# Attention inputs loaded into all 128 partitions, with heads grouped by parity

## The chip, the cores and the metric

The kernel runs on one core of a Trainium2 chip, from Python code that places every instruction on an engine: TensorE (PE) multiplies, ScalarE (ACT) and VectorE (DVE) move and compute, GpSimd (POOL) does some element-wise work, and SyncE (SP) issues the DMAs. The metric is the device time of one launch in microseconds, the median of three runs.

## The reference, cut to what matters

Two attentions, then two mixture-of-experts layers (batch 4, 8 heads, 576 tokens, head size 64, 32 packed queries; 8 experts, width 512, hidden 1024). Everything is float32.

```python
def sm_attn(qq, kk, vv):
    s = scale * np.matmul(qq, kk.transpose(0, 1, 3, 2))
    a = np.exp(s - np.max(s, axis=-1, keepdims=True))
    a = a / (np.sum(a, axis=-1, keepdims=True) + 1e-09)
    return np.matmul(a, vv)
p_packed = sm_attn(p, k, v)              # attention 1: 32 packed queries over 576 tokens
out = sm_attn(q, p_packed, p_packed)     # attention 2: 576 tokens over the 32 packed rows
x = out.transpose(0, 2, 1, 3).reshape(B * S, H * D)
# layer 1: expert = argmax(x @ w_gate); per expert, at most `capacity` tokens:
#   y = relu(x @ w1[e]) @ w2[e], times the token's gate
# layer 2: a second choice of expert with two gates, y = relu(x @ w1b[e]) @ w2b[e]
```

## The kernel before, in words

**Loads.** For each batch, q, k and v come in two halves of four heads each, called G 0 and 1 (`load`, L250). A half is a tile `r` of 96 partitions: partition p holds six consecutive tokens (`R = 6`) of each of the four heads, so a half is 384 pieces of 1536 bytes, 576 KB in all, and there are 24 halves. They rotate through nine buffers (`qkv`). `load_p` brings the packed queries p, 64 KB per batch, and GpSimd copies them next to themselves (`dup_p`). All loads go through SP's queue, which issues in program order and waits there for a free buffer; each load also waits until the load eight places ahead of it has landed.

**Transposes.** `transp` (L257) turns a half of q or k from [96, head, token, d] to [128 = (token parity u, d), 4 heads, 288]: twelve TensorE transposes of [96, 128] into PSUM, then two ACT copies (`evac`, L236) to a tile `T`. For q the copy also reorders columns, so it writes with a step of three elements. `T` has four buffers, one half each.

**Scores.** `score` (L285) makes, for one half, [128 = (4 heads, 32 packed), 2, 288] as eight small matmuls: 64 rows (one token parity) by 32 columns (one head), so that eight tiles of the PE array work side by side. The moving operand is a contiguous run of 288 columns of `T`. A float32 matmul is two instructions in the trace. `s1_mm` does it for k with the packed queries (`pT`), `s2_mm` for q with the packed rows (`ppT`).

**Attention 1's second product.** `s1_exp` writes the weights `a1`, one tile per half. `a1_T` transposes them in six pieces of [128, 96] per half and evacuates on ACT (half 0) or DVE (half 1). `pp_mm` (L326) multiplies with v: 24 matmuls per half of 96 rows by 32 columns with 64 moving columns, four array tiles side by side.

**The rest.** `pp_scale`, `pp_T` normalise and transpose the packed rows; `s2_tr` to `s2_back` are the second softmax, on DVE, POOL and ACT; `g1_*`, `ga` to `gd` choose experts. `moe1_load1` (L491) fetches the chosen expert's w1 as eight loads of 64 partitions (two per 256 columns, one per group of four heads); `moe1_ppw` multiplies it with the packed rows.

**Order.** The order on every engine is written out by hand. `att_iter(b)` runs scores 1 of batch b, the rest of batch b - 1, softmax 2 of batch b - 2. Iterations 0, 1 and 2 are followed by `att_last` (the last scores and the gating of batch 0) and `att_end` (the rest of the last batch, between whose pieces the first expert layer of slot 0 is put). The choice of the first expert, `e0`, is ready near the end of `att_last`; SP then issues w1. Then come the expert layers of two slots, long streams of PE matmuls of 288 or 512 columns.

Of the kernel before, what the change touches and what calls it, by code (L numbers as in the profile page):

```python
# [28 lines left out]
def tile_kernel(  # L29
# [21 lines left out]
    KP = 96  # L51
    R = S // KP
    J = R // 2
    HS = S // 2
# [45 lines left out]
    zt = const.tile([KP, 128], FP32, name="zt")  # L100
# [54 lines left out]
    # ================= gating: pieces =================  # L155
# [3 lines left out]
    def onehot(L, nm, V=nc.vector):  # L159
        """of the logits L [128,n,E]: bf16 one-hot of the first largest, and L less its largest; in two pieces"""  # L160
# [17 lines left out]
    def denom(ex, nm):  # L178
        """1 / (softmax sum + 1e-9)"""
# [7 lines left out]
    def counts(K16, dst):  # L187
        """dst [1,n,E] = kept tokens of each of n batches per expert"""
# [9 lines left out]
    def primary(c, nm, pe, mu, ne, V=nc.vector):  # L198
        """of the counts c [1,n,E]: the index of the largest, more than one?, any?"""
# [50 lines left out]
    def load(b, nm, gs=(0, 1)):  # L250
        src = {"k": k, "q": q, "v": v}[nm]
        for G in gs:
            t = qkv_p.tile([KP, 4, R, D], FP32, tag="r", name="r")
            nc.sync.dma_start(t, src[b, 4 * G:4 * G + 4].rearrange("h (p r) d -> p h r d", r=R))
            raws[nm, b, G] = t

    def transp(b, nm, G, eng=0):  # L257
        """[96, 4 heads, row, d] -> [128 (row parity, d), 4 heads, 288]"""
        src = raws.pop((nm, b, G))
        t = t_p.tile([128, 4, HS], FP32, tag="T", name="T")  # L260
        for hh in range(2):
            ps = psm("tp")
            for u in range(2):
                for j in range(J):
                    tr(nc, ps[:, u, j * KP:(j + 1) * KP], src[:, 2 * hh + u, 2 * j:2 * j + 2, :].rearrange("p r d -> p (r d)"),
                       ident[:KP, :KP])
            i = ps[:, :, 0:HS]
            o = t[:, 2 * hh:2 * hh + 2, :]
            if nm == "q":
                o = o.rearrange("x u (p j) -> x u j p", j=J)  # L270
                i = i.rearrange("x u (j p) -> x u j p", j=J)
            evac(eng, o, i)
        T[nm, b, G] = t

    def make_pT(b):
        pT = ab_p.tile([128, 2, 128], FP32, tag="pT", name="pT")
        ps = psm("pTp")
        for G in range(2):
            tr(nc, ps[:, G, 0:128], p_sb[b][:, G].rearrange("p u d -> p (u d)"), ident)
        nc.scalar.activation(out=pT, in_=ps[:, :, 0:128], func=ACTF.Copy, scale=scale)  # L280
        T["p", b] = pT

    def score(lhs, rhs):
        """lhs(u, hq) [64,32], rhs [128, 4, 288] -> psum [128 (hq, pack), u, 288]"""
        s = psm("s")  # L285
# [14 lines left out]
    def s1_exp(b, G):  # L300
        a1 = at_p.tile([128, 2, HS], FP32, tag="a1", name="a1")
        if G == 0:
            at["sm", b] = as_p.tile([128, 2], FP32, tag="sm", name="sm")
        nc.scalar.activation(out=a1, in_=at.pop(("s1", b, G))[:, :, 0:HS], func=ACTF.Exp,
                             bias=at.pop(("nb", b, G)), accum_out=at["sm", b][:, G:G + 1])
        at["a1", b, G] = a1
# [6 lines left out]
    def a1_T(b, G, eng=0):  # L313
        a1 = at.pop(("a1", b, G))
        ps = psm("a1Tp")
        for u in range(2):
            for j in range(J):
                tr(nc, ps[:KP, u, j * 128:(j + 1) * 128], a1[:, u, j * KP:(j + 1) * KP], ident)
        t = at_p.tile([KP, 2, J, 128], FP32, tag="a1T", name="a1T")
        evac(eng, t, ps[:KP, :, 0:J * 128].rearrange("p u (j n) -> p u j n", j=J))  # L320
        at["a1T", b, G] = t

    def pp_mm(b, G):
        if G == 0:
            at["pp", b] = psm("pp")
        pp, t, vt = at["pp", b], at.pop(("a1T", b, G)), raws.pop(("v", b, G))  # L326
        for u in range(2):
            for j in range(J):
                for hq in range(4):
# [881 lines left out]
```

## Time and profile before

| | |
|---|---|
| time, median of 3 runs | 290.99 us (290.71 to 292.66) |
| span of the profiled execution | 289.3 us |
| PE busy | 259.8 us (90%), 2401 matmuls |
| DVE, ACT, POOL busy | 131.1, 105.4, 44.6 us |
| DMA | 37.16 MB; 50.2% of 16 engines' span |
| packets | 33828, of which 30464 are under 2 KB |

The profiled execution shows only its span, from the first to the last instruction. The median lies 1.7 us above it. A slice of the page is 7.23 us long. A busy PE is not a PE at its peak, since matmuls overlap and the clock may be at half.

### The profile page before, as it was taken

To read this page: it belongs to the slowest core of one execution; us is meant where nothing else is said; L and a number is where in the kernel's file an instruction comes from. 1 tells how busy PE (TensorE), PEld (TensorE's weight loads), DVE (VectorE), ACT (ScalarE), POOL (GpSimd) and SP (SyncE) were. 2 spreads that over 40 slices of the span, in tenths; PEclk is the share of its full clock that TensorE was granted. 3 is DMA by queue.
4 is the path that set the end of the run, shared out by engine and by line. 5 is a ranking of instruction groups with operands and counts; after the bars stand their busy time and mean duration, and the time that the engine had idled before them with its cause. 6 is when DMAs were issued, how large, how long until landed. Compare 5 with 4: busy or idle time off the path is not lost. (4 is left out here: it accounts for less than half of the span.)

```text
span 289.3 us, 5848 instructions
## 1 busy us (share of the span) xinstructions
PE 259.8 (90%) x2401; PEld 226.1 (78%) x2401; DVE 131.1 (45%) x316; ACT 105.4 (36%) x160; POOL 44.6 (15%) x69
## 2 busy tenths in 40 slices
PE   7785949969699898999979999999999999999990
PEld 5565739546479877997879999999888899998870
DVE  0230543858779948617972133359422053640000
ACT  2583537466435412125641224116232143431000
POOL 5000113315415206000533000000010000000100
PEclk9996975998889999999979999999999999999997
DMA  7999999990794000299378622502701181000111
GB/s 176 234 245 199 220 230 239 237 230 9 173 254 160 0 2 0 98 215 227 98 210 227 228 75 72 147 0 76 217 36 54 39 268 61 2 0 36 59 39 44
DMA packets 33828, 37.16 MB, mean 128 GB/s; under 512 B 4224, under 2 KB 30464, under 8 KB 33792
## 3 DMA queue, kind: packets, MB, share of 16 engines
q1 hardware_dynamic: 33792, 36.69, 50.2%
q8 instruction: 21, 0.34, 0.5%
q14 instruction: 15, 0.12, 0.1%
HBM read 31.25 MB, written 4.72 MB: 124 GB/s over the span
## 5 line engine op out<-in xcount | busy, mean ns | idle before, releaser
L21 PE MATMUL o<-w2bh,h 128*128 128x512 f32 x144 | 45.9, 391 | 0.0
L21 PE MATMUL y<-h,w2ah 128*128 128x288 f32 x256 | 44.6, 296 | 0.0
L21 PEld LDWEIGHTS y<-h,w2ah 128*128 128x128 f32 x256 | 37.6, 189 | 0.0
L562 DVE SCALAR_TENSOR_TENSOR h<-h 128x576 fp32r<-128x576 f32 (+3 forms) x64 | 25.8, 446 | 23.6 <-ACT h L555 23.6
L555 ACT ACTIVATE h<-h 128x576 fp32r<-128x576 f32 x32 | 20.4, 650 | 35.0 <-PE h L21 31.2
L25 PE MATMUL tp<-ident,r 96*128 96x96 f32 x192 | 24.1, 290 | 10.0 <-DMA r<-in_q_dram 8.0
L25 PEld LDWEIGHTS tp<-ident,r 96*128 96x128 f32 x192 | 21.8, 172 | 13.5 <-issue 11.0
L21 PEld LDWEIGHTS o<-w2bh,h 128*128 128x128 f32 x144 | 26.9, 188 | 5.7
L21 PE MATMUL o<-w2bl,h 128*128 128x512 f32 x80 | 31.3, 391 | 0.0
L236 ACT ACTIVATE T<-tp 128x576 f32<-128x576 f32 x32 | 24.0, 805 | 19.4 <-PE tp L25 19.2
L21 PE MATMUL y<-h,w2al 128*128 128x288 f32 x128 | 27.6, 297 | 0.7 <-DVE w2al L480 0.7
L21 PE MATMUL h<-yh,w1bh 128*128 128x288 f32 x128 | 27.5, 296 | 0.0
L21 PE MATMUL h<-yh,w1bl 128*128 128x288 f32 x128 | 27.4, 295 | 0.0
L21 PE MATMUL h<-yl,w1bh 128*128 128x288 f32 x128 | 27.3, 295 | 0.0
L21 PEld LDWEIGHTS y<-h,w2al 128*128 128x128 f32 x128 | 20.5, 188 | 1.5 <-DVE w2al L480 1.0
L480 POOL TENSOR_TENSOR w2al<-wraw,w2ah 128x1024 fp32r<-128x1024 f32 x6 | 14.2, 2392 | 44.1 <-DMA wraw<-in_moe_w_dram 26.3
L21 PEld LDWEIGHTS h<-yh,w1bh 128*128 128x128 f32 x128 | 20.6, 189 | 0.2
L21 PEld LDWEIGHTS h<-yh,w1bl 128*128 128x128 f32 x128 | 20.6, 188 | 0.0
L21 PEld LDWEIGHTS h<-yl,w1bh 128*128 128x128 f32 x128 | 20.6, 188 | 0.0
L661 POOL TENSOR_SCALAR osb<-osb,g 64x512 f32<-64x512 f32 x2 | 3.1, 1572 | 110.8 <-DVE osb L660 110.8
L571 ACT ACTIVATE yh<-y 128x576 fp32r<-128x576 f32 x8 | 5.2, 652 | 40.6 <-PE y L21 40.6
L653 ACT ACTIVATE osb<-o,g 128x512 f32<-128x512 f32 x8 | 5.5, 691 | 36.8 <-PE o L21 24.2
(173 smaller groups left out, 387.0 us busy)
## 6 DMA issues: line engine op xcount, KB each, us to landing
wraw<-in_moe_w_dram SPq DMA_DIRECT2D x24, 512.0 KB, 4.8
r<-in_k_dram SPq DMA_DIRECT2D x8, 576.0 KB, 12.4
r<-in_q_dram SPq DMA_DIRECT2D x8, 576.0 KB, 16.4
r<-in_v_dram SPq DMA_DIRECT2D x8, 576.0 KB, 16.4
wraw<-in_moe_w_dram SPq DMA_DIRECT2D x16, 256.0 KB, 5.4
out_dram<-zt SPq DMA_DIRECT2D x2, 1152.0 KB, 7.6
out_dram<-osb SPq DMA_DIRECT2D x8, 256.0 KB, 2.1
a2s<-a2T SPq DMA_DIRECT2D x1, 576.0 KB, 4.9
```

The lines of the kernel that those rows point to most:

```text
L21: return nc.tensor.matmul(out, lhsT=lhsT, rhs=rhs, start=start, stop=stop)
L25: return nc.tensor.transpose(out, in_, ident)
L236: nc.scalar.activation(out=o, in_=i, func=ACTF.Copy)
L480: lo_eng.tensor_tensor(lo, s, hi.bitcast(FP32), op=ALU.subtract)
L555: nc.scalar.activation(out=hi, in_=ps[:, :, 0:HS], func=ACTF.Relu)
L562: nc.vector.scalar_tensor_tensor(o, i, 0.0, a.bitcast(FP32), op0=ALU.max, op1=ALU.subtract)
L571: nc.scalar.activation(out=half(y[0][:, c, :]), in_=ps[:, :, 0:HS], func=ACTF.Copy)
L653: nc.scalar.activation(out=o[:n], in_=ps[:n, 0, :], func=ACTF.Copy, scale=g2[:n, t:t + 1])
L661: nc.gpsimd.tensor_scalar(o[:n], o[:n], g2[:n, t:t + 1], None, op0=ALU.mult)
```

## The change

k and q: a load is now [128, 18, 64]. Partition (h, x) holds 18 of the 36 tokens of block x of head h, one run of 4608 bytes; the two loads of a batch are the two halves of each block, so each holds all eight heads. v: partition (g, p) with g the parity of the head and p a block of nine tokens; a load has four heads, two per parity, in runs of 2304 bytes. Loads keep their number, bytes and place in the program; there are twelve buffers.

A half of q or k is nine transposes of [128, 128], copied contiguously (640 and 512 columns). `T` is one tile per batch and operand, with two buffers. Its columns are (token pair, head, block), so the moving operand of a score, one head's 288 pairs, is read with a step of 128 elements (512 bytes). Every score reads both halves. Heads are grouped by parity: G is now the parity, head = 2 hq + G.

`a1` is one tile for both parities, written by `s1_exp` with a step of two elements. `a1_T` makes nine transposes of [128, 128] per batch, in parts of five and four, whose stationary operand is read with a step of nine elements, and which need both parities. `pp_mm` has 72 matmuls of 64 rows by 32 columns per batch instead of 48 of 96 rows; eight array tiles work side by side.

w1 of the first expert layer is four loads of 128 partitions instead of eight of 64, and `wg_sb` one load instead of two. Comments are removed.

```diff
-    KP = 96
-    R = S // KP
+    ZP = 96
+    BL = 128 // H
+    R = S // BL
     J = R // 2
+    VP = 64
+    VR = S // VP
@@ load_consts
-        for g in range(2):
-            nc.sync.dma_start(
-                wg_sb[64 * g:64 * g + 64], wg1[256 * g:256 * g + 256].rearrange("(q d) e -> d q e", d=64))
+        nc.sync.dma_start(wg_sb, wg1.rearrange("(c p) e -> p c e", p=128))
@@ pools
-    qkv_p = apool("qkv", 9)
-    t_p = apool("t", 4)
+    qkv_p = apool("qkv", 12)
+    t_p = apool("t", 2)
+    a1t_p = apool("a1t", 1)
@@ load_p
-        nc.sync.dma_start(t[:, :, 0, :], p[b].rearrange("(g q) n d -> (q n) g d", g=2))
+        nc.sync.dma_start(t[:, :, 0, :], p[b].rearrange("h (x y) d -> (h x) y d", y=2))
@@ load, transp
-            t = qkv_p.tile([KP, 4, R, D], FP32, tag="r", name="r")
-            nc.sync.dma_start(t, src[b, 4 * G:4 * G + 4].rearrange("h (p r) d -> p h r d", r=R))
+            t = qkv_p.tile([128, J, D], FP32, tag="r", name="r")
+            if nm == "v":
+                nc.sync.dma_start(
+                    t.rearrange("p (q r) d -> p q (r d)", q=2),
+                    v[b, 4 * a:4 * a + 4].rearrange("(q g) (p r) d -> (g p) q (r d)", g=2, r=VR))
+            else:
+                nc.sync.dma_start(
+                    t, (k if nm == "k" else q)[b].rearrange("h (x r) d -> (h x) r d", r=R)[:, J * a:J * a + J, :])
-        t = t_p.tile([128, 4, HS], FP32, tag="T", name="T")
-                    tr(nc, ps[:, u, j * KP:(j + 1) * KP], src[:, 2 * hh + u, 2 * j:2 * j + 2, :].rearrange("p r d -> p (r d)"),
-                       ident[:KP, :KP])
+            T[nm, b] = t_p.tile([128, J, 128], FP32, tag="T", name="T")
+        pair = src.rearrange("p (j u) d -> p j (u d)", u=2)
+        for r0, r1 in ((0, 5), (5, VR)):
+            ps = psm("tp").rearrange("p u n -> p (u n)")
+            for r in range(r0, r1):
+                tr(nc, ps[:, (r - r0) * 128:(r - r0 + 1) * 128], pair[:, r], ident)
+            evac(eng, t[:, VR * a + r0:VR * a + r1, :].rearrange("p r x -> p (r x)"), ps[:, 0:(r1 - r0) * 128])
@@ score, s1_mm
-                mm(nc, s[32 * hq:32 * hq + 32, u, 0:HS], lhs(u, hq), rhs[64 * u:64 * u + 64, hq, :], True, True)
+                mm(nc, s[32 * hq:32 * hq + 32, u, 0:HS], lhs(u, hq), rhs(u, hq), True, True)
+        pT, kT = T["p", b], T["k", b].rearrange("p j (h x) -> p h x j", h=H)
+            lambda u, hq: kT[64 * u:64 * u + 64, 2 * hq + G])
@@ s1_exp, a1_T, pp_mm
+            at["a1", b] = at_p.tile([128, 2, HS, 2], FP32, tag="a1", name="a1")
+        nc.scalar.activation(out=at["a1", b][:, G].rearrange("p c u -> p u c"), in_=at.pop(("s1", b, G))[:, :, 0:HS],
+        a1 = at["a1", b].rearrange("p g c u -> p (g c u)").rearrange("p (x r) -> p r x", r=VR)
+        for r in range(r0, r1):
+            tr(nc, ps[:, (r - r0) * 128:(r - r0 + 1) * 128], a1[:, r], ident)
+        for r in range(*PARTS[i]):
+            for hq in range(4):
+                for G in range(2):
+                    g = slice(64 * G, 64 * G + 64)
+                    mm(nc, pp[32 * hq:32 * hq + 32, G, 0:D], t[g, r, 32 * hq:32 * hq + 32], vt[hq // 2][g, hq % 2, r, :],
+                       r == 0, r == VR - 1)
@@ moe1_load1
-            for G in range(2):
-                nc.sync.dma_start(
-                    w[64 * G:64 * G + 64],
-                    w1a[bass.ds(e, 1), 256 * G:256 * G + 256, fq * 256:(fq + 1) * 256].rearrange(
-                        "o (q d) f -> d (o q) f", d=64),
-                )
+            nc.sync.dma_start(
+                w, w1a[bass.ds(e, 1), :, fq * 256:(fq + 1) * 256].rearrange("o (q p) f -> p (o q) f", p=128))
```

Where the program's order and waits move, two places show it. The first is SP's queue, from the loads of batch 1's q and v on (`DMAHW` is the landing of the load eight ahead, `PE` a buffer that TensorE must have read). Before:

```order
L254 DMA r<-in_q_dram 96x4x384 [waits DMAHW2_49,PE_49]
L254 DMA r<-in_v_dram 96x4x384 [waits DMAHW3_49,PE_49]
L254 DMA r<-in_v_dram 96x4x384 [waits DMAHW4_49,PE_49]
L254 DMA r<-in_q_dram 96x4x384 [waits DMAHW5_49,PE_49]
L244 DMA p_sb<-in_p_dram 128x2x64 [waits DMAHW6_49,Pool_49]
L254 DMA r<-in_k_dram 96x4x384 [waits DMAHW7_49,PE_49]
```

And now:

```order
L262 DMA r<-in_q_dram 128x1152 [waits DMAHW1_49]
L258 DMA r<-in_v_dram 128x2x576 [waits DMAHW2_49]
L258 DMA r<-in_v_dram 128x2x576 [waits DMAHW3_49]
L262 DMA r<-in_q_dram 128x1152 [waits DMAHW4_49,PE_49]
L248 DMA p_sb<-in_p_dram 128x2x64 [waits DMAHW5_49,PE_49,Pool_49]
L262 DMA r<-in_k_dram 128x1152 [waits DMAHW6_49,PE_49]
```

The first load that needs a buffer back from TensorE moves from the first half of batch 1's q to its second half, three loads later.

The second place is PE's queue in iteration 1, from the second part of batch 0's `a1_T` to its product with v. Before (`a_295` is `a1`, `s` scores 1 of batch 1, `tp` batch 0's second half of q, `pp` the product):

```order
L25 MATMUL a1Tp<-ident,a_295 96x128 [waits Activation_49]
L25 MATMUL a1Tp<-ident,a_295 96x128 x5
L21 MATMUL s<-T,pT 32x288 [waits Activation_49]
L21 MATMUL s<-T,pT 32x288 x7
L25 MATMUL tp<-ident,r 128x96 [waits DMAHW1_49,Activation_49]
L25 MATMUL tp<-ident,r 128x96 x5
L25 MATMUL tp<-ident,r 128x96 [waits Activation_49]
L25 MATMUL tp<-ident,r 128x96 x5
L21 MATMUL pp<-r,a1T 32x64 [waits DMAHW7_49,DVE_49]
L21 MATMUL pp<-r,a1T 32x64 x23
L21 MATMUL pp<-r,a1T 32x64 [waits DMAHW0_49]
L21 MATMUL pp<-r,a1T 32x64 x23
```

And now:

```order
L25 MATMUL a1Tp<-ident,a_276 128x128 [waits Activation_49]
L25 MATMUL a1Tp<-ident,a_276 128x128 x3
L21 MATMUL s<-T,pT 32x288 [waits Activation_49]
L21 MATMUL s<-T,pT 32x288 x7
L25 MATMUL tp<-ident,r 128x128 [waits DMAHW1_49,Activation_49]
L25 MATMUL tp<-ident,r 128x128 x4
L25 MATMUL tp<-ident,r 128x128 [waits DVE_49]
L25 MATMUL tp<-ident,r 128x128 x3
L21 MATMUL pp<-r,a1T 32x64 [waits DMAHW7_49,Activation_49]
L21 MATMUL pp<-r,a1T 32x64 x3
L21 MATMUL pp<-r,a1T 32x64 [waits DMAHW0_49]
L21 MATMUL pp<-r,a1T 32x64 x67
```

The steps stand in the same order. Transposes are fewer and wider, the product has 72 matmuls instead of 48, and it waits for the second load of v after its fourth matmul instead of its twenty-fourth.

## Rows read from the trace of the kernel before

**Rows 1.** Page, part 2: 40 slices of the span; granted clock in tenths, GB/s.

```profile
PEclk9996975998889999999979999999999999999997
...
GB/s 176 234 245 199 220 230 239 237 230 9 173 254 160 0 2 0 98 215 227 98 210 227 228 75 72 147 0 76 217 36 54 39 268 61 2 0 36 59 39 44
```

**Rows 2.** Stretches: PE, PEld, DVE, ACT, POOL busy us (count), clock, DMA share, GB/s.

```profile
0.00:65.00 65.00, 50.21 (x768) 38.61 (x769) 23.58 (x56) 33.04 (x56) 12.97 (x50) 0.86 1.04 223
75.00:82.00 7.00, 5.41 (x72) 3.02 (x73) 5.01 (x13) 2.56 (x4) 3.27 (x4) 0.76 1.08 219
...
159.00:161.00 2.00, 2.00 (x17) 2.00 (x16) 0.34 (x1) 0.00 (x0) 0.00 (x0) 1.00 1.00 342
```

**Rows 3.** Waits of PE, 0 to 72 us: who, total us, times, longest.

```profile
PE tp L25 <- DMA r<-in_q_dram: 8.0, 2, 4.3
PE pp L21 <- issue: 2.3, 1, 2.3
PE tp L25 <- DMA r<-in_k_dram: 1.9, 2, 1.0
...
PE pTp L25 <- POOL p_sb L248: 1.0, 1, 1.0
```

**Rows 4.** Timeline, iterations 0 and 1: start, us, engine, line, what, count [idle before].

```profile
5.73 2.15 PE L25 MATMUL tp<-ident,r 96*128 96x96 f32 x12 [1.01 <-DMA r<-in_k_dram]
...
9.22 2.16 PE L25 MATMUL tp<-ident,r 96*128 96x96 f32 x12 [0.90 <-DMA r<-in_k_dram]
...
11.30 2.06 PE L21 MATMUL s<-T,pT 64*32 64x288 f32 x32
...
17.12 0.82 PE L25 MATMUL a1Tp<-ident,a 128*96 128x128 f32 x6
...
24.78 2.15 PE L25 MATMUL tp<-ident,r 96*128 96x96 f32 x12 [3.75 <-DMA r<-in_q_dram]
...
26.86 2.79 PE L21 MATMUL pp<-r,a1T 96*32 96x64 f32 x96
```

**Rows 5.** Timeline, iteration 2 to the first loads of w1.

```profile
34.62 0.72 PE L21 MATMUL s<-T,pT 64*32 64x288 f32 x16
...
35.26 1.21 PE L25 MATMUL tp<-ident,r 96*128 96x96 f32 x12
...
42.10 2.15 PE L25 MATMUL tp<-ident,r 96*128 96x96 f32 x12 [4.29 <-DMA r<-in_q_dram]
...
47.39 2.13 PE L25 MATMUL tp<-ident,r 96*128 96x96 f32 x12
...
49.73 1.62 PE L25 MATMUL tp<-ident,r 96*128 96x96 f32 x12
...
58.01 0.88 PE L21 MATMUL pp<-r,a1T 96*32 96x64 f32 x48
...
64.57 1.52 PE L25 MATMUL a1Tp<-ident,a 128*96 128x128 f32 x6
...
72.57 1.45 SPq L498 DMA_DIRECT2D wraw<-in_moe_w_dram  x2
```

**Rows 6.** A stretch after the first wait for q; columns as rows 2.

```profile
25.00:30.00 5.00, 5.00 (x110) 4.61 (x110) 0.28 (x2) 2.54 (x4) 0.29 (x1) 0.50 0.92 150
```

**Rows 7.** ACT's copies of k (first), q (second): count, min/median/max ns.

```profile
L236 ACT ACTIVATE T<-tp x4: 645/652/652, 48.6 to 51.5; 128x576 f32<-128x576 f32 x4
...
L236 ACT ACTIVATE T<-tp x2: 957/962/966, 19.3 to 20.1; 128x576 f32<-128x576 f32 x2
```

**Rows 8.** Timeline of PE in the first expert layer of slot 1.

```profile
159.84 0.42 PE L21 MATMUL y<-h,w2al 128*128 128x288 f32 x2
160.10 0.69 PE L21 MATMUL y<-h,w2ah 128*128 128x288 f32 x4
160.63 0.43 PE L21 MATMUL y<-h,w2al 128*128 128x288 f32 x2
```

**Rows 9.** Waits of PE's weight loads, 72 us to the end.

```profile
PEld ppw L21 <- DMA wraw<-in_moe_w_dram: 2.3, 3, 1.1
```

More of the change, by code (lines that the diff above doesn't have):

```diff
@@ L99, in tile_kernel @@
         nc.gpsimd.memset(iob[:, b:b + 1], float(b))
-    zt = const.tile([KP, 128], FP32, name="zt")
+    zt = const.tile([ZP, 128], FP32, name="zt")
     nc.gpsimd.memset(zt, 0.0)
@@ L248, in dup_p, with load @@
         nc.gpsimd.tensor_copy(p_sb[b][:, :, 1, :], p_sb[b][:, :, 0, :])
-    def load(b, nm, gs=(0, 1)):
-        src = {"k": k, "q": q, "v": v}[nm]
-        for G in gs:
-            t = qkv_p.tile([KP, 4, R, D], FP32, tag="r", name="r")
-            nc.sync.dma_start(t, src[b, 4 * G:4 * G + 4].rearrange("h (p r) d -> p h r d", r=R))
-            raws[nm, b, G] = t
-    def transp(b, nm, G, eng=0):
-        src = raws.pop((nm, b, G))
-        t = t_p.tile([128, 4, HS], FP32, tag="T", name="T")
[L261 to L264, printed above, removed]
-                    tr(nc, ps[:, u, j * KP:(j + 1) * KP], src[:, 2 * hh + u, 2 * j:2 * j + 2, :].rearrange("p r d -> p (r d)"),
-                       ident[:KP, :KP])
[L267 to L273, printed above, removed]
+    def load(b, nm, pieces=(0, 1)):
+        for a in pieces:
+            t = qkv_p.tile([128, J, D], FP32, tag="r", name="r")
[6 more added lines that the diff above has]
+                    t, (k if nm == "k" else q)[b].rearrange("h (x r) d -> (h x) r d", r=R)[:, J * a:J * a + J, :])
+            raws[nm, b, a] = t
@@ L275, in make_pT @@
     def make_pT(b):
-        pT = ab_p.tile([128, 2, 128], FP32, tag="pT", name="pT")
+        pT = ab_p.tile([128, H, 2, NP // 2], FP32, tag="pT", name="pT")
         ps = psm("pTp")
-        for G in range(2):
-            tr(nc, ps[:, G, 0:128], p_sb[b][:, G].rearrange("p u d -> p (u d)"), ident)
-        nc.scalar.activation(out=pT, in_=ps[:, :, 0:128], func=ACTF.Copy, scale=scale)
+        for y in range(2):
+            tr(nc, ps[:, y, 0:128], p_sb[b][:, y].rearrange("p u d -> p (u d)"), ident)
@@ L281, in make_pT @@
+        nc.scalar.activation(
+            out=pT.rearrange("p h y x -> p y h x"), in_=ps[:, :, 0:128].rearrange("p y (h x) -> p y h x", h=H),
+            func=ACTF.Copy, scale=scale)
         T["p", b] = pT
@@ L300, in s1_exp @@
     def s1_exp(b, G):
[L301 removed]
         if G == 0:
+            at["a1", b] = at_p.tile([128, 2, HS, 2], FP32, tag="a1", name="a1")
             at["sm", b] = as_p.tile([128, 2], FP32, tag="sm", name="sm")
[L304 to L306 removed]
+        nc.scalar.activation(out=at["a1", b][:, G].rearrange("p c u -> p u c"), in_=at.pop(("s1", b, G))[:, :, 0:HS],
+                             func=ACTF.Exp, bias=at.pop(("nb", b, G)), accum_out=at["sm", b][:, G:G + 1])
     def s1_rs(b):
@@ L311, in s1_rs, with a1_T, pp_mm @@
         nc.vector.reciprocal(sm, sm)
[L313 to L324, printed above, removed]
-            at["pp", b] = psm("pp")
[L326 to L329, printed above, removed]
-                    mm(nc, pp[32 * hq:32 * hq + 32, G, 0:D], t[:, u, j, 32 * hq:32 * hq + 32],
-                       vt[:, hq, 2 * j + u, :], u == 0 and j == 0, u == 1 and j == J - 1)
+    PARTS = ((0, 5), (5, VR))
+    def a1_T(b, i, eng=0):
+        if i == 0:
+            at["a1T", b] = a1t_p.tile([128, VR, 128], FP32, tag="a1T", name="a1T")
+        r0, r1 = PARTS[i]
+        a1 = at["a1", b].rearrange("p g c u -> p (g c u)").rearrange("p (x r) -> p r x", r=VR)
+        ps = psm("a1Tp").rearrange("p u n -> p (u n)")
+        for r in range(r0, r1):
+            tr(nc, ps[:, (r - r0) * 128:(r - r0 + 1) * 128], a1[:, r], ident)
+        evac(eng, at["a1T", b][:, r0:r1].rearrange("p r x -> p (r x)"), ps[:, 0:(r1 - r0) * 128])
+    def pp_mm(b, i):
+        if i == 0:
+            at["pp", b] = psm("pp")
+        pp, t = at["pp", b], at["a1T", b]
+        vt = [raws["v", b, a].rearrange("p (q r) d -> p q r d", q=2) for a in range(2)]
+        for r in range(*PARTS[i]):
[4 more added lines that the diff above has]
+                       r == 0, r == VR - 1)
     def pp_scale(b):
```

17 lines of the change are left out of this document (11 added, 6 removed).

## The prediction, made before the changed kernel ran

> **What bounds the kernel now.** I read the page's 40 slices first [rows 1]. The loads run flat at about 200 to 245 GB/s in the first nine slices and then stop, while the clock dips in slices 4, 6 and 7 and again around 11. From about 75 us on the clock stays at nines. So there are two kernels in one: an attention that runs beside a saturated load queue, and an expert part in which PE has work all the time. The stretches say how saturated [rows 2]: 0 to 65 us has a DMA share of 1.04 and only 223 GB/s. 24 loads of 589,824 bytes and four p of 64 KB are 14.4 MB; at 223 GB/s that is 65 us, the whole stretch.
>
> Next the waits of PE up to 72 us [rows 3]: 8.0 us for q in two waits, 2.3 us ahead of the product with v (an "issue" wait, where v of batch 2 is the operand still missing), 1.9 us for k, 1.0 us for p. That is 13.2 us. [...]
>
> **The loads.** The same 16 engines at the same share reach very different rates: 223 GB/s at 1.04 for pieces on 96 partitions, 219 at 1.08 for w1 on 64 partitions, 342 at 1.00 for weights on 128 partitions, although those pieces are shorter (1 KB) [rows 2]. No row shows pieces of 2304 or 4608 bytes from memory, so the rate lies between no gain (223) and 342 or somewhat more; I take 342, the row with the same number of partitions. Then a load takes 1.72 us instead of 2.6, and all 14.4 MB take 42 us instead of 65.
>
> *Start.* The first load lands 0.9 us earlier, so the transposes of 5.73 us start at 4.83, and those of 9.22 at 7.4, where PE gets there and not the load. Scores now need both copies of k, one more copy of 0.65 us [rows 7]. So the scores of 11.30 us start at 7.4 + 2.08 + 0.65 = 10.1, 1.15 us earlier; the wait for p (0.95 in the timeline) goes as well. Iteration 1 (17.12 us, rows 4) starts 2.1 us earlier.
>
> *Waits for q and v.* 3.75 and 4.29 us [rows 4, 5] and 2.3 us [rows 3] go, if the loads are in time. Taking 3.1 us as the first load's start of transfer (4.83 - 1.72): the eighth load lands at 17.3 us and is wanted at 18.9; the fourteenth at 27.8, wanted at 29.8; v of batch 2 (the nineteenth) at 36.6, wanted at 43.9; the last at 45, wanted at 54. The margins close at about 315 GB/s; at 280 the fourteenth is 3.5 us late and the later ones are not later than that. SP no longer holds these back: the first load that wants a buffer from PE is three places later, and deeper buffers leave the rest well ahead.
>
> *Half clock.* After the first wait: 2.15 - 1.21 for 12 transposes, 2.79 - 2 x 0.88 for the product [rows 4, 5], and 0.2 for two small transposes (estimate), 2.2 us. After the second: the transposes of 42.10, 47.39 and 49.73 us give back 0.94 + 0.92 + 0.41 [rows 5], the product the same 1.03 (it has the same 96 instructions), small ones 0.5 (estimate), 3.8 us. After the third, six transposes at 64.57 us take 1.52 instead of 0.82 [rows 4, 5]: 0.7 us.
>
> Sum: 2.1 + 3.75 + 2.2 + 4.29 + 3.8 + 2.3 + 0.7 = 19.1 us.
>
> *w1.* Eight loads of 64 partitions become four of 128: 2.1 MB at 342 instead of 219 GB/s, 6.1 instead of 9.6 us. In slot 0 the weight loads of PE wait 2.3 us for w1 [rows 9]; I take 1.0 of it, since DVE's and ACT's work for the last batch stands next to these waits. In slot 1 no wait on w1 shows, and nothing is gained. The shorter SP queue gains nothing either.
>
> **PE's own work, which is now the bound.** *Transposes of q and k:* 24 narrow ones per operand and batch took 2 x 1.21 us; 18 wide ones, by six wide ones in 0.82 us [rows 4], take up to 2.46. I take no change. *`a1_T`:* 12 become 9, 1.64 becomes 1.23 us, so -1.6 us over four batches. The strided stationary operand has no row; its bounds are nothing and a doubling of the 1.23 us (+4.9 in all). I take nothing, since weight loads lie beside other matmuls. *`pp_mm`:* 144 instructions per batch instead of 96. At the present pace, 48 in 0.88 us [rows 5], that is 2.64 instead of 1.76 us; if eight tiles side by side finish twice as many as four, it is 1.3. So -0.4 to +0.9 per batch; I take +0.6, near the upper end, because 64 columns are so short that the number of instructions counts, +2.4 in all.
>
> *Strided scores.* This is the unknown. 16 scores of 16 instructions each take 0.72 us now [rows 5]. A stream of 288 columns alone takes 0.79 / 6 = 0.13 us [rows 8]. If the step of 512 bytes costs nothing, a score stays at 0.72. If the tiles could no longer read side by side at all, it is 16 x 0.13 = 2.1 us. The nearest row with a step is another engine's: ACT's copies of q write with a step of 12 bytes and take 962 instead of 652 ns [rows 7], 1.5 times. If each stream takes 1.5 to 2 times 0.13 us and the tiles still overlap, a tile's two streams end 0.13 to 0.26 us later. I take +0.25 per score, 4.0 in all, with 0 and 22 us as bounds.
>
> [...]
>
> *ACT.* 16 copies of q lose 0.31 us each, 5.0 us; eight `s1_exp` write with a step and may gain as much each, at most 2.5 us. I cost both at nothing: the second `s1_exp` of a batch is followed by k's transposes before `a1_T` wants it. Without that cover it is 0.3 us for each of four batches. *New waits:* with loads early, PE meets ACT, DVE and POOL more often, whose copies and second softmax had slack during the waits for q. I allow 1.5 us (estimate: a score's 0.72 us for each of two iterations).
>
> **Sum.** 19.1 + 1.0 - (2.4 - 1.6) - 4.0 - 1.5 = 13.8 us. The expert part behind it moves as a whole. The span goes from 289.3 to 275.5; with the 1.7 us between the span and the median of the runs, 277.
>
> **Rivals.** *A, the strided read halves the score's pace:* a score takes 1.44 instead of 0.72 us, as if only half of the tiles could read at once. 16 x 0.72 = 11.5 instead of 4.0, and the time is 284.7. For it: eight tiles draw on the same rows of memory at once, four of them on the same 64 partitions. Against it: the present 0.72 us is mostly start and end of the streams. [...]
>
> *B, the loads don't get faster:* 223 GB/s is what this stream from memory can do. Then only w1's and PE's small terms move and the time stays within 1%, about 290. For it: no row has 14 MB in one go at 342. Against it: the share of 1.04 at 223 says the engines are busy and slow, while 1.00 goes with 342.
>
> *C, slower:* the tiles of a score read one after the other. Without the strided term the gain is 17.8 us; it is used up when a score takes 0.72 + 17.8 / 16 = 1.83 us. At 2.1 us, with 16 instructions in a row at 0.13, the price is 22 us and the time 295. [...] Against it: the row with a step loses a factor of 1.5, not three.
>
> *D, better than forecast:* the strided read is free and no new waits come, 271.5; with eight tiles also faster in the product, 267.5.
>
> **Chances.** The forecast, with a range of its own of 270 to 283 (the lower end without strided price, the upper end with the loads at 280 GB/s): 0.62. A 0.15, D below 270 0.14, B 0.05, C 0.04. A run of this kernel tells about 1% from no change, so faster means below 288.1: forecast, A and D, 0.91. Within 1%: B, 0.05. Slower: C, 0.04. The range of 266 to 287 leaves out B, C, the upper part of A and the lower part of D, under 0.2.
>
> **What would show it.** In the profile after: the stretch of loads ends near 45 us at about 340 GB/s; no wait of PE for q or v over 1 us and a clock of 1.00 from 20 to 60 us; iteration 1 starts near 15 us and w1 is issued near 55 to 60 us (72.57 now); a score of 16 instructions takes 0.9 to 1.0 us; 72 product matmuls take about 2.3 us a batch. The prediction is wrong if a score takes over 1.4 us, if the loads stay under 280 GB/s, or if PE waits for ACT or DVE by more than 3 us in an iteration.

## The result, and the profile after

The changed kernel takes 279.99 us (279.18 to 280.06), the kernel before 291.83 us beside it; the ratio is 0.961 (95% 0.955 to 0.966). 277.0 was forecast, within 266 to 287. The profiled execution has a span of 278.1 us, 11.2 less than before; 13.8 less were forecast. Two profiles further down, of runs for k and of the loads of 64 partitions, are of the longest execution of their kernels (277.5 and 289.7 us), so lengths read from them lean long.

The page's slices after (the rows that answer to [rows 1]):

```profile
PEclk9999999998899999999799999999999999999998
...
GB/s 220 386 328 332 401 394 32 5 5 215 241 154 0 2 0 49 307 206 75 210 158 302 125 78 101 52 0 162 142 45 49 53 303 26 4 0 38 61 40 45
```

The loads take six slices instead of nine, at 220 to 400 GB/s, and the dips of the clock at 20 to 55 us are gone; eights stay in slices 10 and 11 (63 to 76 us). By stretches (columns as in [rows 2]):

```profile
0.00:43.00 43.00, 37.20 (x597) 23.79 (x597) 14.69 (x35) 24.16 (x45) 9.77 (x46) 1.00 0.94 338
30.00:35.00 5.00, 5.00 (x62) 2.40 (x51) 3.78 (x8) 1.59 (x3) 1.12 (x1) 1.00 1.03 408
```

At the DMA share that gave 223 GB/s before [rows 2], 408 are moved; the mean from 0 to 43 us is 338. The waits of PE in the first 75 us (compare [rows 3]):

```profile
PE ppTp L25 <- DVE pps L349: 1.8, 1, 1.8
PE tp L25 <- DMA r<-in_k_dram: 1.7, 2, 1.5
PE s L21 <- ACT T L240: 1.5, 2, 0.8
PE s L21 <- issue: 1.3, 1, 1.3
PE gp L21 <- issue: 1.2, 1, 1.2
...
PE ppw L21 <- DMA wraw<-in_moe_w_dram: 0.2, 1, 0.2
```

No wait for q is left, and v and p are not waited for. But two waits called "issue" stand there, 2.5 us together. The timeline of PE (compare [rows 4, 5]):

```profile
4.89 1.95 PE L25 MATMUL tp<-ident,r 128*128 128x128 f32 x9 [0.17 <-DMA r<-in_k_dram]
8.54 1.17 PE L25 MATMUL tp<-ident,r 128*128 128x128 f32 x9 [1.49 <-DMA r<-in_k_dram]
10.56 2.64 PE L21 MATMUL s<-T,pT 64*32 64x288 f32 x32 [0.84 <-ACT T L240]
...
16.08 0.74 PE L25 MATMUL a1Tp<-ident,a 128*128 128x128 f32 x5
17.47 1.42 PE L21 MATMUL s<-T,pT 64*32 64x288 f32 x16 [0.66 <-ACT T L240]
18.83 1.20 PE L25 MATMUL tp<-ident,r 128*128 128x128 f32 x9
...
31.16 0.85 PE L25 MATMUL a1Tp<-ident,a 128*128 128x128 f32 x5
...
37.42 1.66 PE L21 MATMUL pp<-r,a1T 64*32 64x64 f32 x144
...
47.09 0.84 PE L25 MATMUL a1Tp<-ident,a 128*128 128x128 f32 x5
```

A score takes 1.42 us where it took 0.72. The product has 144 instructions in 1.66 us, where 96 took 2 x 0.88. Iteration 1 starts at 16.08 (17.12 before), iteration 2 at 31.16 (33.83), the last scores' stage at 47.09 (54.41), and the first matmul of the expert layers at 70.35 (81.07). So the first stage is 1.0 us shorter, iteration 1 1.6, iteration 2 4.7, the last stage 3.4, the experts 0.5: 11.2 us in all.

### The profile page after: what moved, and what is told of

It reads as the page before. It is cut to its first block, busy times and chain, and to the rows that moved or that the text cites. A ratio compares the mean times of both kernels' runs of the same rounds, so it can differ in the third digit from the quotient of the medians.

```text
span 278.1 us, 6072 instructions
## 1 busy us (share of the span) xinstructions
PE 258.7 (93%) x2533; PEld 218.1 (78%) x2533; DVE 130.7 (47%) x316; ACT 100.8 (36%) x160; POOL 44.7 (16%) x69
## 4 chain that ended last, share of the span: by engine, by line
PE 79%; DVE 10%; DMA 4%; ACT 2%; issue 2%; SPq 1%; POOL 0%; ACTq 0%; DVEq 0%; POOLq 0%
PE h L21 23%; PE o L21 18%; PE y L21 17%; PE s L21 7%; PE tp L25 4%; DMA r<-in_k_dram 2%; PE pp L21 2%; DVE eq L206 2%; PE l L21 2%; DVE h L572 2%; PE lp L21 1%; PE a1Tp L25 1%; DMA wraw<-in_moe_w_dram 1%; PE ppw L21 1%; ACT T L240 1%
## 5 line engine op out<-in xcount | busy, mean ns | idle before, releaser
L240 ACT ACTIVATE T<-tp 128x640 f32<-128x640 f32 (+1 forms) x32 | 19.0, 652 | 15.0 <-PE tp L25 15.0
L25 PEld LDWEIGHTS tp<-ident,r 128*128 128x128 f32 x144 | 16.5, 146 | 8.7 <-issue 2.9
L25 PE MATMUL tp<-ident,r 128*128 128x128 f32 x144 | 19.7, 284 | 1.7 <-DMA r<-in_k_dram 1.7
```

The costliest lines, as they stand in the source:

```text
L25: return nc.tensor.transpose(out, in_, ident)
L240: nc.scalar.activation(out=o, in_=i, func=ACTF.Copy)
```

## The experiments

Two questions come out of this. Is it the step of 512 bytes that doubled the score, and what would its return bring? And what are the waits called "issue", one of which the prediction had put down to v? The theory: the step alone makes the score slow, the partitions alone make the loads fast, and PE waits for its own code. All kernels are edits of the changed one. The median of the kernel before was 290.1 to 292.1 us beside them, so times and ratios to before compare to about 1%: 0.961 is the changed kernel's ratio, and 0.962 when it was run again with the last experiments.

One thing moves a time whatever the edit. From the first expert matmul to the end, where the work is the same, the two profiles of the changed kernel take 207.8 and 205.6 us. TensorE waits 2.38 us for DVE at 134 us in both; behind that wait the granted clock is 0.50 for some 3 us in the first profile and 1.00 in the second:

```profile
136.50:139.50 3.00, 3.00 (x13) 3.00 (x14) 2.40 (x11) 1.16 (x3) 0.00 (x0) 0.50 0.99 255
136.50:139.50 3.00, 3.00 (x25) 3.00 (x24) 2.12 (x11) 1.44 (x3) 0.20 (x1) 1.00 0.95 246
```

Seven of the fourteen profiles have it (the kernel before among them; expert part 207.6 to 209.0 us), seven don't (205.6 to 205.9). So less than about 2 us between two profiles is not yet an effect of an edit.

### Runs of 16 columns for all scores

```diff
-        pT, kT = T["p", b], T["k", b].rearrange("p j (h x) -> p h x j", h=H)
+        pT, kT = T["p", b], T["k", b].rearrange("p j (h x) -> p h j x", h=H)
@@ s1_exp
-   out=at["a1", b][:, G].rearrange("p c u -> p u c"), in_=s[:, :, 0:HS]
+   out=at["a1", b][:, G].rearrange("p (x j) u -> p u j x", j=J), in_=s[:, :, 0:HS].rearrange("p u (j x) -> p u j x", j=J)
@@ the same for qT in s2_mm, and in s2_back
+   a2T[:, b, G].rearrange("p (x n jj u) -> p u n jj x", n=NB2, jj=2, u=2)
```

> The scores read T in another column order: 16 columns that lie side by side (one head's blocks of one token pair), then a step to the next pair, so that 18 runs of 64 bytes replace 288 columns at a step of 512 bytes. The new order is undone where the weights are written: s1_exp writes runs of a1 with a step of 144 bytes between elements, s2_back writes a2T by pieces. Theory (the 512-byte step is what makes a score 1.43 us): a score of 16 instructions falls to 0.72 to 0.85 us, and the 16 scores give back 16 x 0.6 to 0.7 = 9.6 to 11.4 us; the time is 269 to 272 against 280, a little above if the writes of s1_exp (0.78 to 0.96 us now) get longer. Rival 1 (it is not the step but the larger tile, read by two operands' halves, or that both halves must be there): the score stays at 1.4 us, and the time at 280. Rival 2 (PE's own score is no longer what sets the iteration): the score falls, but waits of PE for ACT or DVE take the place of it, and the time is 277 to 280.

277.46 us, ratio 0.960 (0.938 to 0.981). The score is back, the time hardly. Timeline of PE:

```profile
16.66 0.72 PE L21 MATMUL s<-T,pT 64*32 64x288 f32 x16 [0.61 <-ACT T L240]
...
24.85 0.72 PE L21 MATMUL s<-T,ppT 64*32 64x288 f32 x16
27.88 0.20 PE L21 MATMUL gp<-wg_sb,ppT 64*32 64x8 f32 x3 [2.29 <-issue]
...
29.49 1.21 PE L21 MATMUL s<-T,pT 64*32 64x288 f32 x16
30.64 2.09 PE L25 MATMUL tp<-ident,r 128*128 128x128 f32 x9
```

and, from 10 to 70 us, DVE's and ACT's groups that write by the new order (count, busy us, mean ns):

```profile
L400 DVE STREAM_TRANSPOSE a2T<-sT 128x576 f32<-128x576 f32 x4 | 4.8, 1190 | 0.0
```

```profile
L312 ACT ACTIVATE a<-s,nb 128x576 f32<-128x576 f32 x8 | 10.4, 1318 | 1.8 <-DVE nb L305 1.8
```

0.72 us ahead of the wait at 27.9 us, as before the change [rows 5]: the step is the whole cause of the doubling, and rival 1 falls. The gain goes into three things. The wait called "issue" in iteration 1 grows from 1.2 to 2.3 us. After it PE is slow for some microseconds (2.09 us for nine transposes that take 1.20, 1.21 us for a score; the mean granted clock of the execution is 0.972, against 0.984 in the changed kernel). And the strides come back on the other engines: `s1_exp` from 0.85 to 1.32 us, `s2_back` from 0.80 to 1.19, and TensorE's waits for them grow: 2.2 instead of 0.5 us behind the last transposes for DVE, 0.9 us instead of none for `s1_exp`. That is rival 2 in its time and in a part of its cause: the wait called "issue" and the slow stretch were not in it.

### Runs for k alone, and an `s1_exp` that reads with the step

The first kernel undoes only k's part of the edit above (k scores in runs, q's with the step).

> The same for the eight scores of k alone; those of q keep the step of 512 bytes. Theory: the k scores fall to 0.72 to 0.85 us, the q scores stay at 1.43, and half of the gain appears, 4.8 to 5.7 us, 274 to 275. Rival (the k scores are covered by waits elsewhere, and q's set the time, or the reverse): a gain of less than 2 us, or nearly the whole of what both bring.

275.67 us, ratio 0.953 (0.930 to 0.976). The k scores take 0.72 us and q's 1.42; iterations 1 and 2 last 13.8 and 14.9 us instead of 15.1 and 15.9. Half of the edit brings as much as the whole, as far as the intervals tell. The second kernel also turns the order of `s1_exp`'s elements:

```diff
-   out=at["a1", b][:, G].rearrange("p (x j) u -> p u j x", j=J), in_=s[:, :, 0:HS].rearrange("p u (j x) -> p u j x", j=J)
+   out=at["a1", b][:, G].rearrange("p (x j) u -> p x j u", j=J), in_=s[:, :, 0:HS].rearrange("p u (j x) -> p x j u", j=J)
```

> Like the kernel with runs of 16 columns for k's scores, but s1_exp puts its elements in the other order: it writes a1 in its own order without a step and reads the scores in PSUM with a step. There s1_exp took 1.32 us writing with steps of 144 bytes, against 0.85 us in the changed kernel (steps of 8 bytes) and 0.65 us that ACT takes for 576 columns without a step. Theory (ACT pays for steps where it writes, not where it reads PSUM): s1_exp takes 0.65 to 0.85 us, the waits of k's transposes for it (0.3 us twice) go, and the time is 1 to 2 us below the kernel with runs for k, 273.5 to 274.5. Rival (it pays for any step): 1.3 us or more, and no gain.

272.65 us, ratio 0.936 (0.924 to 0.948), a little better than expected; its interval overlaps that of the kernel with runs for k. ACT's group:

```profile
L312 ACT ACTIVATE a<-s,nb 128x576 f32<-128x576 f32 x8 | 6.0, 745 | 2.3 <-DVE nb L305 2.3
```

The same permutation costs 1.32 us as a strided write and 0.75 us as a strided read of PSUM (steps of 2 KB and 64 bytes).

### q's scores without a step, by q's copies

```diff
+            if nm == "q":
+                evac(eng, t.rearrange("p j c -> p (j c)").rearrange("p (c j) -> p c j", j=J)[:, :, VR * a + r0:VR * a + r1],
+                     ps[:, 0:(r1 - r0) * 128].rearrange("p (r c) -> p c r", c=128))
-        qT = T["q", b].rearrange("p j (h x) -> p h x j", h=H)
+        qT = T["q", b].rearrange("p j c -> p (j c)").rearrange("p (h n) -> p h n", h=H)
```

> On top of the kernel with runs for k and an s1_exp that reads with a step: q's copies from PSUM now put the columns in the order (head, block, token pair), reading PSUM with a step of 512 bytes and writing runs of 5 or 4 elements, so that the q scores read 288 columns in one run, and the second softmax stays as it is. Theory (the score pays only for its own step; a copy that reads PSUM with a step pays little, as s1_exp did, 0.75 instead of 0.65 us): q scores fall from 1.43 to 0.72 us, the copies of q take 0.6 to 0.85 us, and of the 5.7 us of the eight q scores 2 to 4 us show in the time, since waits for code and for DVE take some back: 269 to 271. Rival (a copy that writes short runs pays as the q copies before the change, 0.96 us and more, and PE waits for ACT): 272 to 274, no gain.

274.38 us, ratio 0.943 (0.937 to 0.949): no gain over 0.936, so the rival's time, but not by its cause. q's scores take 0.72 us, and the copies pay almost nothing (0.75 and 0.64 us over those of k and q, against 0.71 and 0.60). PE waits for its queue instead:

```profile
PE warm L21 <- DVE sT L376: 1.6, 1, 1.6
...
PE s L21 <- issue: 1.2, 1, 1.2
...
PE tp L25 <- issue: 1.1, 1, 1.1
PE gp L21 <- issue: 0.5, 1, 0.5
PE pp L21 <- issue: 0.5, 1, 0.5
```

3.3 us of "issue" against 1.7 in the kernel with k's runs, and 1.6 us for the second softmax on DVE against 0.8. That is 2.4 of the 5.7 us; where the rest went was not settled. Of the 2.8 us between the two spans, 2.3 lie in the expert part (208.1 against 205.8 us), which the edit does not touch; up to it the kernel with q's copies is 0.5 us behind.

### What "issue" is: TensorE's code

In the changed kernel the two waits lie behind 689 and 1194 recorded instructions of TensorE, in the kernel with runs behind the same counts, and in the kernel before [rows 3] behind 1445. Near each, the DMA part of the profile shows a transfer of 16 KB by a queue called instruction. The link is tight: over all fourteen profiles TensorE has 34 waits called "issue" of over 0.15 us, and each ends 1.2 to 1.6 us behind the end of such a transfer, wherever it stands in the program. The transfers also go with the count: from 92.7 to 238.9 us of the changed kernel there are eight, for 2063 recorded instructions of TensorE. That is 258 for each 16 KB, some 64 bytes an instruction (estimate: 16384 bytes by 258 are 63.5); the theory takes 256. In the stretch from 27 to 29 us of the changed kernel (packets, MB, share of 16 engines):

```profile
q1 hardware_dynamic: 324, 0.72, 99.2%
q8 instruction: 1, 0.02, 3.1%
```

PE stands still from 28.6 to 29.8 us. The test moves the program against these counts, without changing its work:

```diff
-        warm(16)
+        warm(9)
+        ps = psm("warm")
+        for _ in range(57):
+            mm(nc, ps[0:32, 0, 0:8], wz[:, 0:32], wz[:, 0:8], True, True)
```

> Nothing of the computation changes. TensorE gets 57 tiny matmuls (32 columns by 8, 114 instructions) in the idle time before its first transposes, and 7 fewer of the warming matmuls (14 instructions), so that every later instruction stands 100 places later in its queue. The cause to be tested: the two waits of 1.2 and 1.3 us that the profile calls issue lie, in the changed kernel, in the runs-only kernel and in the four-tiles kernel alike, behind the same counts of recorded TensorE instructions, 689 and 1194; a 16 KB transfer of the queue called instruction (256 instructions of 64 bytes) ends 1.2 to 1.3 us before each goes on; and from the crossing of the place 256 earlier to the end of the wait it is 6.1 to 6.5 us. Theory (PE waits for its code, 256 instructions at a time): the borders now fall 100 instructions earlier in the program, at recorded counts 590 and 1095 of the old numbering, just inside the product's 288 instructions; the earlier border is passed at 23.0 instead of 23.6 us and the later one is wanted at 24.9 instead of 28.6 us, so the wait grows from 1.2 to about 4.3 us in iterations 1 and 2 each, and lies inside the product with v; the time is 284 to 288 instead of 280. Rival (the wait belongs to a semaphore of ACT or DVE at that place of the program): both waits stay at 1.2 to 1.3 us ahead of the same instructions, and the time stays at 280.

283.04 us, ratio 0.971 (0.961 to 0.980). The waits, in the timeline of PE:

```profile
29.07 0.37 PE L25 MATMUL pTp<-ident,p_sb 128*128 128x128 f32 x1 [3.76 <-issue]
...
45.51 0.41 PE L21 MATMUL pp<-r,a1T 64*32 64x64 f32 x19 [1.45 <-issue]
```

They stand behind 693 and 1198 recorded instructions again, which are now other places of the program: behind and within the product. So they belong to the count and not to a semaphore, and 100 more instructions without work cost 3 us by the medians (the kernel with w1 in eight loads, below, took 279.99 on the same chip). Not all of it is code: the second transposes of k took 2.15 instead of 1.17 us for nine in this profile (2.07 in that of nine buffers, 2.15 in that of the kernel with runs and nine buffers), and iteration 1 starts 0.6 us later; iteration 1 itself lasts 19.7 instead of 15.1 us. The second wait was forecast at 4.3 and is 1.45 us, and the time stays below the 284 to 288 us expected. From the place 256 recorded instructions earlier to the end of the wait it is 5.6 us for the first (23.5 to 29.1) and 2.9 us for the second (42.6 to 45.5); the stretches of the two differ in the DMA share (clock, DMA share and GB/s at the end):

```profile
25.00:30.00 5.00, 1.24 (x10) 1.02 (x7) 0.61 (x2) 0.41 (x2) 0.00 (x0) 0.80 1.02 391
30.00:35.00 5.00, 5.00 (x51) 3.90 (x50) 0.67 (x3) 2.63 (x4) 0.29 (x1) 0.52 1.03 404
40.00:45.00 5.00, 4.06 (x152) 2.44 (x150) 2.77 (x6) 4.55 (x10) 2.57 (x3) 1.00 0.65 186
```

In the changed kernel the same stretch takes 6.2 us for the first wait (23.6 to 29.8, DMA share 1.02) and 6.1 for the second (37.9 to 44.0, share 0.71); what sets its length was not shown. The first wait of the shifted kernel was also followed by a granted clock of 0.52 (30 to 35 us, above). The longest, 3.76 us, stands beside full engines (1.02), but these are not needed for a wait: the kernels with runs have one of 0.4 to 1.1 us in the last stage, behind a product, when the loads are over. In the kernel with q's copies it is the 1.1 us ahead of `tp` above, at 47.6 to 48.7 us:

```profile
45.00:48.70 3.70, 2.59 (x127) 2.34 (x125) 2.10 (x8) 2.04 (x4) 0.44 (x2) 1.00 0.02 4
```

In these waits that stretch takes 3.1 to 3.8 us (in this one 252 recorded instructions from 45.0 to 48.7 us).

### What makes the loads fast

One kernel brings k and q in pieces of 1536 bytes, the old length, on all 128 partitions; the other keeps 4608 bytes and halves each load's partitions.

```diff
@@ short pieces
-   t, ...rearrange("h (x r) d -> (h x) r d", r=R)[:, J * a:J * a + J, :]
+   t.rearrange("p (c r) d -> p c (r d)", c=3), ...rearrange("h (x r) d -> (h x) r d", r=R).rearrange("p (c a r) d -> p a c (r d)", c=3, a=2)[:, a]
@@ 64 partitions
+   for h0 in range(0, 128, 64):
+       t[h0:h0 + 64], ...rearrange("h (x r) d -> (h x) r d", r=R)[h0:h0 + 64, J * a:J * a + J, :]
```

> The loads of q and k keep their 128 partitions, but bring three pieces of 1536 bytes per partition instead of one of 4608 (the length of a piece in the kernel before, which went to 96 partitions). v is unchanged. Transposes are in parts of six and three, their copies put the tokens where they stood. Theory (the partitions make the rate): the stretch from 10 to 40 us still moves 340 to 400 GB/s, the last load lands by 48 us, no wait of PE for q above 1 us, time 280 to 282. Rival (the length of the pieces makes the rate): q and k come at about 223 GB/s as before the change, the loads end near 58 us, waits for q of 2 to 4 us come back, and the time is 286 to 290.

> Each load of k and q is cut into two loads of 64 partitions (four heads each) that SP issues one after the other; pieces of 4608 bytes, bytes, order and everything else stay. Theory (the number of partitions that a load covers makes its rate): the stretch of 10 to 40 us moves about 220 to 260 GB/s, as loads on 64 and 96 partitions did before the change, the loads end at 55 to 62 us, waits of PE for q of 2 to 4 us come back, and with them stretches at half clock; the time is 286 to 292. Rival (transfers of two halves run side by side and fill the engines together): 380 to 400 GB/s as in the changed kernel, and 280 to 281 us.

Short pieces: 282.0 us, ratio 0.981 (0.963 to 0.998). 64 partitions: 287.57 us, ratio 0.983 (0.972 to 0.995). Stretches of the first:

```profile
35.00:40.00 5.00, 4.83 (x168) 3.26 (x166) 3.55 (x7) 4.31 (x8) 2.53 (x3) 1.00 1.05 375
```

and of the second:

```profile
10.00:15.00 5.00, 3.92 (x44) 1.39 (x42) 1.51 (x2) 2.04 (x4) 0.29 (x1) 1.00 1.05 221
...
35.00:40.00 5.00, 5.00 (x56) 2.49 (x50) 4.37 (x8) 2.72 (x5) 0.00 (x0) 1.00 1.04 212
```

The old piece length costs some 7% of the rate (375 against 401 GB/s in the same stretch) and no wait for q; its time is 2 us higher by the medians, 3 above the four-tiles kernel below, run on the same chip, and 5.8 by the ratios; the intervals don't separate them. Half of the partitions costs half of the rate at the same share, brings waits for q and k back (1.1 and 3.9 us, where the changed kernel has none and 1.7; below the 2 to 4 us expected for q), doubles the waits for code (5.2 instead of 2.5 us), ends the loads at 64 us and takes away 6.5 (by the ratios) to 7.6 us (by the medians) of the gain. Packets say the same: 1536 bytes took a median of 109 ns on 96 partitions and 66 on 128; 4608 bytes took 178 ns on 128 and 331 on 64. The partitions make the rate, but not in proportion: 96 of them gave 223 GB/s [rows 2], no more than 64 do here, and no run tells why, nor why 64 give half of what 128 do.

### Parts that do little

Four tiles in a row of one parity, then four of the other, in the product:

```diff
-            for hq in range(4):
-                for G in range(2):
+            for G in range(2):
+                for hq in range(4):
```

> The product with v in another order: for each token block, the four matmuls of parity 0 and then the four of parity 1, instead of the parities in turn. Instructions and bytes are the same. Theory 1 (the pace of 11 to 12 ns per matmul instruction comes from rows 0 to 63 and 64 to 127 of the array working in turn): with four in one half after another, 144 instructions take 2.0 to 2.64 us instead of 1.66 to 1.80, and the time is 281 to 283. Theory 2 (the pace belongs to the shorter matmul of 64 rows, in any order): 1.7 us as now, and the time is 280.

278.98 us, ratio 0.970 (0.950 to 0.989). The timeline of PE has

```profile
24.33 1.66 PE L21 MATMUL pp<-r,a1T 64*32 64x64 f32 x144
```

as in the other order: theory 1 falls. Whether the pace of 11 to 12 ns comes from 64 rows instead of 96, as theory 2 has it, or from eight tiles instead of four was not tested apart.

w1 in eight loads of 64 partitions again:

```diff
+            for G in range(2):
                 nc.sync.dma_start(
-                w, w1a[bass.ds(e, 1), :, fq * 256:(fq + 1) * 256].rearrange("o (q p) f -> p (o q) f", p=128))
+                w[64 * G:64 * G + 64], w1a[...].rearrange("o (q g d) f -> g d (o q) f", g=2, d=64)[G])
```

> w1 of the first expert layer comes again as eight loads of 64 partitions instead of four of 128. The prediction took 1.0 us for this edit in slot 0 and nothing in slot 1. Theory: the product of w1 and the packed rows waits for w1 again, 1.0 to 2.3 us, while DVE and ACT have work beside it, and the time is 280.5 to 281.5. Rival (the wait is covered): waits appear, but the first matmul of the hidden layer starts at the same distance behind the issue of w1 (6.8 us now, 8.5 before), and the time is 280.

279.99 us, ratio 0.960 (0.951 to 0.970): no difference in the time. In its profiled execution the product with w1 waits 0.7 instead of 0.2 us, and the hidden layer starts 9.0 us behind the issue of w1 instead of 6.8. Neither statement of the expectations covers both; the edit is worth between 0 and 2.3 us.

Nine buffers instead of twelve, and the changed kernel itself beside it:

```diff
-    qkv_p = apool("qkv", 12)
+    qkv_p = apool("qkv", 9)
```

> Nine buffers for k, q and v instead of twelve. Theory (with loads at 340 to 400 GB/s SP is held by the landing of the load eight places ahead, not by buffers): no wait of PE for q or v over 1 us, the loads end before 47 us, time 280. Rival (loads wait for buffers that v holds until the product): loads end after 50 us, a wait for q or v of 1 to 3 us, time 281 to 284.

> The changed kernel itself, beside the others on one chip, to have its time there: 280, ratio to before 0.96, by every theory; the second transposes of k start between 8.1 and 9.2 us, scores take 1.43 us, and two waits called issue of 1.1 to 1.4 us stand in iterations 1 and 2.

277.75 us, ratio 0.956 (0.952 to 0.961), against 279.53 us, ratio 0.962 (0.957 to 0.967). No wait for q or v in either. With nine buffers the loads thin out earlier and end later (191 and 249 GB/s in slices six and seven, against 395 and 30), a little past the 47 us of the theory, and nothing waits for them; the three more buffers bring nothing. In the changed kernel's second profile the two waits for code are 1.8 and 0.2 us, where 1.4 or less for the first and 1.1 or more for the second were expected: they shift from run to run.

### The best of them

Runs for k, `s1_exp` reading with the step, nine buffers:

> The two edits that cost nothing or gained, together: runs of 16 columns for k's scores with an s1_exp that reads with a step and writes without one, and nine buffers. Theory (the two are independent, and nine buffers change nothing by themselves): the time of the kernel with runs for k alone, 271 to 273, ratio to before 0.93 to 0.94. Rival (the lower time of the kernel with nine buffers, 277.75 against 279.53, is a gain of its own): 269.5 to 271.

274.21 us (272.59 to 274.45), ratio 0.946 (0.940 to 0.952). It is no better than with twelve buffers (0.936, 0.924 to 0.948), so the rival falls, and the time lies above what the theory said. Both beat the changed kernel, by 1.5 to 2.5% (0.946 and 0.936 against 0.961).

## Why the prediction was right, and where it was not

The bound was read rightly: loads at 223 GB/s with the engines full, and PE paying for them in waits and then in stretches at a granted clock of 0.50. The total is near because several terms were wrong in opposite directions: 6.5 us too little for the scores and 2.5 for the "issue" wait, against 2.3, 2.2 and 1.2 us that the last stage, the product with `a1_T` and the expert part gave beyond the forecast. That part is luck. Measured terms are differences of the stages above, with the score's and the waits' rows taken out:

| term, us | forecast | measured |
|---|---|---|
| start, without scores | -2.1 | -1.6 |
| waits for q | -8.0 | -8.0 |
| half clock | -6.7 | -7.1 |
| "issue", taken for v | -2.3 | +0.2 |
| w1 and the last stage | -1.0 | -3.3 |
| product and `a1_T` | +0.8 | -1.4 |
| strided scores | +4.0 | +10.5 |
| new waits for ACT | +1.5 | +0.7 |
| expert part, without its score | 0 | -1.2 |
| sum | -13.8 | -11.2 |

**Loads, waits for q, half clock: right.** 342 GB/s were taken from the row with the same partitions; 401 to 408 came where the stretches are full of loads, and the kernels with short pieces and with 64 partitions show that the partitions were the main reason. They ended at 43 us (45 forecast); the clock is 1.00 from 20 to 60 us. The half-clock term is what iterations 1 and 2 lost beyond waits and scores, 2.2 and 4.2, and 0.7 after the third; in the kernel before the granted clock was 0.50 from 25 to 30 us [rows 6], 42 to 50 and 64.5 to 66.1 us. The sentence that the clock stays at nines from about 75 us on reads [rows 1] wrongly: slices 10 to 12 (65 to 87 us) are eights. No term rests on it.

**Start: a load too late.** The second transposes start at 8.54 instead of 7.4 us, and the load sets that, not PE: 1.5 to 2.2 us of wait for k in most profiles. So iteration 1 starts 1.0 us earlier, 1.6 without the scores' price.

**Strided scores: the step costs, but not as taken.** The estimate of 1.5 to 2 times the stream of 0.13 us, overlapping, gave +0.25 us; +0.70 was measured, rival A's price to the hundredth (1.42 to 1.44 us). What failed is the overlap: not the end of a score but the whole score doubled, and each of its matmuls nearly so (median 768 and 774 ns, 404 and 415 before). By the prediction's own sign, a score over 1.4 us, it was wrong here. ACT's factor of 1.5 was no measure for TensorE, and why it is just two was not tested. The sum of 10.5 instead of 11.4 has the first two scores at +0.58 for both, since they had taken 2.06 us together before [rows 4]. Runs of 64 bytes cost nothing (0.72 us), a step of 512 bytes for each element doubles the score; whether only half of the tiles read at once, as A had it, was not shown.

**v: the step that failed.** The prediction read the 2.3 us "issue" wait ahead of the product as v of batch 2. In the timeline of PE in the kernel before it is this row:

```profile
62.33 0.55 PE L21 MATMUL pp<-r,a1T 96*32 96x64 f32 x25 [2.31 <-issue]
```

It lies in the middle of the product, behind 1445 recorded instructions, not at a place where the product waits for v, and a 16 KB transfer of the instruction queue ends at 60.7 us, 1.6 us before it goes on. So faster loads could not remove it as such. It went from that place, and 1.2 and 1.3 us came at two others. The place 256 recorded instructions ahead of each of them (23.6 and 37.9 us) lies within the product, whose 288 instructions, matmuls and weight loads, now pass in 1.7 us. The count agrees: two 16 KB transfers and 505 recorded instructions from one wait to the other. The changed kernel has 22 such transfers and only these two waits of PE called "issue"; those listed above show up to 3.8 us.

**Product, `a1_T`, transposes.** +0.6 a batch for the product was too much: 144 instructions take 1.66 to 1.80 us (the table has 1.66) against 1.76 for 96. The strided stationary operand costs nothing that shows (five and four in 0.74 and 0.62 us; five contiguous ones took 0.77 in the kernel with runs for all scores); `a1_T` gave 0.25 a batch, not 0.4. Wide transposes take 1.15 to 1.20 us, as taken.

**w1: undersized, and not settled.** 3.3 us is what the last stage lost beyond its five scores, code, clock and product, and not all of it is w1; in the kernel before, the product there also waited for ACT, and the expert part, which lost 1.2 us, for a weight of its own. Neither wait is left:

```profile
71.41 0.88 PE L21 MATMUL pp<-r,a1T 96*32 96x64 f32 x48 [0.58 <-ACT a1T L236]
97.57 0.53 PE L21 MATMUL y<-h,w2al 128*128 128x288 f32 x2 [0.74 <-DVE w2al L480]
```

The kernel with eight loads gives back 2.3 us in its profile and nothing in its median. w1 is issued at 63.58 us, later than the 55 to 60 that was to be seen; 14 of the slower scores and both waits for code stand before it.

**Rivals.** B, C and D are out: 408 GB/s, 1.42 us a score, 280 us. A's price for a score came true and its time, 284.7, did not: other terms paid for it. Undoing the step brings less than the 10.5 us: 4 to 7 us with k's half and a faster `s1_exp`, and nothing more with q's half, of whose 5.7 us code and DVE take 2.4.

## What to carry to other kernels

Price a transfer by the partitions that it covers before the length of its pieces (all 128 here gave nearly twice what 96 or 64 gave: 401 to 408 GB/s against 223 and 212 to 221), and a strided matmul operand by a row of its own engine, not by another engine's (twice the time on TensorE here, 1.5 times on ACT). If an order has to be permuted, do it where PSUM is read (0.75 us here, 1.32 as a strided write), and keep what is written and what TensorE streams in runs. A wait called "issue" at the same instruction count in several kernels was code here: count instructions, not only time, where many small matmuls stand together, above all beside full DMA queues (3.76 us at a share of 1.02).

## What the runs showed of the hardware that was not expected

- A moving operand with a step of 512 bytes doubles a score of eight tiles (0.72 to 1.43 us); runs of 16 columns (64 bytes) between such steps cost nothing (0.72 us). A stationary operand with a step of 36 bytes costs nothing that shows (0.74 us for five transposes, 0.77 without the step).
- ACT for 576 columns: 0.75 us reading PSUM with steps of 2 KB and 64 bytes, 0.85 us writing with 8 bytes, 1.32 us writing with 144 bytes. DVE's transpose goes from 0.80 to 1.19 us when it writes by pieces.
- Where TensorE waits for its code, it is 5.6 and 6.2 us from the place 256 recorded instructions earlier to the end of the wait at a DMA share of 1.02, 6.1 us at 0.71, 2.9 us at 0.65 and 3.1 to 3.8 us with the loads over (0.02). It goes on 1.2 to 1.6 us behind the end of a 16 KB transfer of the queue called instruction.
- Eight matmul tiles of 64 rows take 11 to 12 ns per instruction where four tiles of 96 rows took 18, in either order of the tiles.
- The same wait of 2.38 us for DVE is followed by some 3 us at a granted clock of 0.50 in one execution and of 1.00 in another.
